# Moving fourteen K masks from GpSimd to VectorE, and making the instruction order with measured GpSimd lengths

## The chip, the cores and the metric

The kernel runs on one core of one Trainium2 chip. A time is the device time of one execution in microseconds (us). Most executions of one kernel agree within some tenths of a per cent. The profile is one further look at an execution, taken by the hardware profiler; its span is a little shorter than the device time (284.9 us against 286.6 for the kernel before).

Names in the profile: PE is TensorE's matmuls, PEld its weight loads, DVE is VectorE, ACT is ScalarE, POOL is GpSimd, SP is SyncE. L738 is line 738 of the kernel.

## The reference

The input x is 2048 x 512. Two branches read it and a gate mixes them:

```python
g = sigmoid((x * gate_w).sum(-1, keepdims=True))
a = attention(x)        # 32 heads of 16, in 4 segments of 512 rows, each segment causal,
                        # plus a recurrent memory M, z carried from segment to segment, then @ wo
b = (relu(x @ W_gate) * (x @ W_up)) @ W_down      # 1792 hidden columns
out = g * a + (1 - g) * b
```

Inside a segment the attention is `softmax(q @ k.T * scale + mask) @ v`. The dense products (q, k, v, gate, up, down, wo) are most of TensorE's work. The attention needs every engine: scores on TensorE, exponentials on ScalarE, the causal triangle masks on GpSimd, the product with v ("PV") on TensorE again, then transposes and scaling on VectorE.

## The kernel before

The program is written as a list of small operations. Each has a table "engine: assumed length in us", dependencies and buffers. A list scheduler in the kernel's own source simulates the engines with these lengths and fixes the order in which instructions are issued. At run time each engine executes its instructions strictly in that order. A wrong length makes no wrong result; it makes an order in which an engine stands at an instruction that is not ready while later ones are.

The odd and even heads of a pair share 32 partitions, so K is masked twice, once for each (`r` is 0 for the even heads, 1 for the odd):

```python
for r, mc in ((0, mcole), (1, mcol)):
    def f(e, r=r, mc=mc):
        (nc.vector if e == "DVE" else nc.gpsimd).tensor_scalar(                     # L552, L553
            k2.t[:, :, r, :], k.t[:].rearrange("p (b k) -> p b k", k=64), mc[:, 0:1], None, ALU.mult)
    o_k2[s, c].append(op(f"k2{s}{c}{r}",
                         {"DVE": 0.45} if r == 0 or (s == 0 and c < 2) else {"POOL": 0.8}, f, ...))
```

There are 4 segments `s` and 4 groups `c` of eight heads, so 16 odd masks; two are on VectorE already, 14 on GpSimd.

The triangle masks come after the exponentials (two instructions a part, 128 parts, 256 instructions):

```python
for off in offs:
    for r in range(2):
        v = eb_.t[64 * r:64 * r + 64, :, off:off + 64]
        nc.gpsimd.affine_select(out=v, in_=v, compare_op=ALU.is_ge, fill=0.0, ...)   # L738
m = op(f"m{s}{c}.{n}", {"POOL": 0.8 * len(parts)}, f, deps=[b], ...)
```

PV waits for all of these masks of its unit. Its result goes through VectorE's transposes and products; in segments 1 to 3 a GpSimd add then joins it with the memory part, and VectorE transposes the sum:

```python
Oa.t[:] = Oa.t[:] + Ob.t[:]     # L895: op "ad", {"POOL": 0.8} for 11 of 12, the last {"DVE": 0.5}
nc.vector.transpose(dst.t[:], Oa.t[:]...)                                            # L899
```

PSUM holds one score tile and four tiles G that all other matmuls share. VectorE and ScalarE empty them. So when VectorE stands at an instruction, TensorE soon stands too, for want of a free G.

The softmax here doesn't subtract the row's maximum and nothing guards it: scores larger than these inputs give would overflow.

## Time and profile before

| | before |
|---|---|
| median, three runs | 286.34 us (284.88 to 286.56) |
| profiled span | 284.9 us |
| TensorE busy | 265.1 us, 93% |
| GpSimd busy | 210.7 us, 74% |
| ScalarE, VectorE busy | 194.0 us, 179.7 us |
| mean granted TensorE clock | 0.982 |

The profile's page for the kernel before: busy time and share of the span by engine, then busy tenths and granted clock in 40 slices of 7.1 us.

```profile
PE 265.1 (93%) x2626; PEld 119.0 (42%) x2661; DVE 179.7 (63%) x402; ACT 194.0 (68%) x188; POOL 210.7 (74%) x481
...
PE   8999999978979989999799997999999899999995
...
POOL 9299889989889886799858988648988886636000
PEclk9999999997999999999899997999999999999999
```

TensorE is the busiest, but its row has holes, and the clock row drops where some holes are. GpSimd is at 8 or 9 tenths in most slices of the middle. (35 matmuls fewer than weight loads are listed: some records are missing, so TensorE's idle time of 284.9 - 265.1 = 19.8 us is overstated, by 2 to 3 us as an estimate: the waits view has 2.6 us of idle time marked "issue".)

The groups of instructions of the kernel before (line, engine, operation, output <- input, shapes, count | busy us, mean ns of one | idle before them and what ended it):

```profile
L738 POOL TENSOR_SCALAR_AFFINE_SELECT E<-E 64x256 bf16<-64x256 bf16 x256 | 115.9, 453 | 30.9 <-ACT E L730 16.8
L553 POOL TENSOR_SCALAR K<-KT,mcol 128x512 bf16<-128x512 bf16 x14 | 22.2, 1591 | 6.0 <-ACT KT L509 5.1
L895 POOL TENSOR_TENSOR O<-O,O 128x512 bf16<-128x512 bf16 x11 | 12.8, 1161 | 4.6 <-DVE O L873 4.0
...
L553 DVE TENSOR_SCALAR K<-KT,mcole 128x512 bf16<-128x512 bf16 x16 | 7.2, 447 | 0.5 <-ACT KT L509 0.5
L553 DVE TENSOR_SCALAR K<-KT,mcol 128x512 bf16<-128x512 bf16 x2 | 0.7, 348 | 0.0
```

The same mask takes 1591 ns on GpSimd and 348 ns on VectorE. The scheduler believed 0.8 us for it, 0.8 us for two triangle masks that take 2 x 453 ns, and 0.8 us for an add that takes 1161 ns.

Who waited for whom, the kernel before (us in total, times, longest):

```profile
DVE oT L899 <- POOL O L895: 18.4, 10, 3.4
...
PE G L818 <- POOL E L738: 4.0, 4, 2.6
PE G L242 <- DVE T L853: 2.5, 3, 1.0
PE G L242 <- DVE hT L641: 2.0, 1, 2.0
```

The timeline of the kernel before around its longest TensorE gap, GpSimd's queue first (start us, duration us):

```profile
53.39 1.56 POOL L553 TENSOR_SCALAR K<-KT,mcol 128x512 bf16<-128x512 bf16 x1
54.90 0.88 POOL L472 COPY R<-rcol 32x4 f32<-32x4 f32 x4
55.85 2.02 POOL L738 TENSOR_SCALAR_AFFINE_SELECT E<-E 64x256 bf16<-64x256 bf16 x4
57.94 2.32 POOL L472 COPY R<-rcol 32x4 f32<-32x4 f32 x8
...
64.53 1.82 POOL L738 TENSOR_SCALAR_AFFINE_SELECT E<-E 64x256 bf16<-64x256 bf16 x4
64.99 0.37 PE L818 MATMUL G<-E,Vp 64*32 64x256 bf16 x4 [2.64 <-POOL E L738]
```

Here PV waits 2.64 us for triangle masks, which stand in a queue that was never empty. The second kind of gap goes through VectorE:

```profile
137.23 1.15 POOL L895 TENSOR_TENSOR O<-O,O 128x512 bf16<-128x512 bf16 x1
138.41 0.71 DVE L899 STREAM_TRANSPOSE oT<-O 128x512 bf16<-128x512 bf16 x1 [3.44 <-POOL O L895]
139.05 1.85 DVE L641 TENSOR_TENSOR hT<-G,rg 128x512 bf16<-128x512 f32 x3
139.75 0.64 PE L242 MATMUL G<-xT,wg_sb 128*128 128x512 bf16 x2 [1.99 <-DVE hT L641]
```

VectorE stands 3.44 us at a transpose behind GpSimd's late add; the product hT behind it, which would free a G, is late; TensorE stands 1.99 us.

The granted clock falls to half at three places of this trace, for 3.4 us each (from 65.1, 140.2 and 174.3 us): right after the two longest gaps, 2.64 and 1.99 us, and after a stretch of shorter ones, 0.95, 0.16 and 0.21 us. Stretches of 2 us around the first (busy us of PE, PEld, DVE, ACT and POOL with instruction counts, then clock, DMA share, GB/s):

```profile
62.00:64.00 2.00, 0.35 (x24) 0.09 (x1) 0.37 (x1) 2.00 (x3) 1.70 (x7) 1.00 0.18 37
64.00:66.00 2.00, 0.90 (x32) 0.60 (x31) 0.00 (x0) 0.46 (x1) 1.71 (x6) 0.77 0.14 28
66.00:68.00 2.00, 1.78 (x18) 0.50 (x12) 1.75 (x3) 0.00 (x0) 1.76 (x5) 0.50 0.00 0
```

TensorE works again from 65 us, at half clock up to 68.5 us. Over the whole span a mean clock of 0.982 is (1 - 0.982) x 284.9 = 5.1 us of full-speed work lost.

### The profile page before, as it was taken

The numbers are of one execution on the slowest core, as the hardware profiler recorded it, in microseconds if no ns is written. First come the engines' busy times: TensorE is split into PE (matmuls) and PEld (weight loads), VectorE is DVE, ScalarE is ACT, GpSimd is POOL, SyncE is SP. The second block draws the span as 40 slices with busy tenths as digits, with TensorE's granted clock in tenths as the row PEclk, the third lists the DMA queues.
The fourth block names the chain that finished last, engine by engine and source line by source line (L and its number), as shares of the span: only waits on it lengthen the run. The fifth ranks groups of instructions, "written<-read, shape, count | busy, mean of one in ns | idle before, by whom it ended". The sixth has DMA issues, their size and how long they took to land.

```text
span 284.9 us, 6734 instructions
## 1 busy us (share of the span) xinstructions
PE 265.1 (93%) x2626; PEld 119.0 (42%) x2661; DVE 179.7 (63%) x402; ACT 194.0 (68%) x188; POOL 210.7 (74%) x481
## 2 busy tenths in 40 slices
PE   8999999978979989999799997999999899999995
PEld 6444444423444434444245433344434444444444
DVE  1498778975685527799477941848697645456601
ACT  3599879983857565999678562788868756777010
POOL 9299889989889886799858988648988886636000
PEclk9999999997999999999899997999999999999999
DMA  6992990023600000001531000000000001100011
GB/s 185 290 226 61 317 305 9 2 51 72 101 5 18 21 18 21 0 2 21 141 45 21 21 18 21 20 0 2 3 0 2 2 1 39 38 2 0 2 37 39
DMA packets 27600, 15.52 MB, mean 54 GB/s; under 512 B 13616, under 2 KB 27568, under 8 KB 27568
## 3 DMA queue, kind: packets, MB, share of 16 engines
q1 hardware_dynamic: 26736, 14.63, 20.0%
q10 hardware_dynamic: 832, 0.46, 0.5%
q8 instruction: 21, 0.34, 0.5%
q14 instruction: 11, 0.09, 0.1%
HBM read 9.84 MB, written 2.10 MB: 42 GB/s over the span
## 4 chain that ended last, share of the span: by engine, by line
PE 58%; POOL 27%; issue 6%; DVE 5%; ACT 3%; POOLq 0%; DVEq 0%; ACTq 0%
PE G L242 44%; POOL E L738 12%; PE S L716 5%; PE G L818 4%; POOL R L472 3%; POOL CM L792 3%; POOL K L553 2%; POOL O L895 2%; ACT E L730 2%; PE G L240 2%; PE S L402 1%; POOL M L618 1%; DVE T L853 1%; PE G L285 1%; DVE hT L641 1%
## 5 line engine op out<-in xcount | busy, mean ns | idle before, releaser
L730 ACT ACTIVATE E<-S 128x2048 bf16<-128x2048 f32 x72 | 135.0, 1875 | 48.7 <-PE S L716 44.6
L738 POOL TENSOR_SCALAR_AFFINE_SELECT E<-E 64x256 bf16<-64x256 bf16 x256 | 115.9, 453 | 30.9 <-ACT E L730 16.8
L242 PE MATMUL G<-xT,wg_sb 128*128 128x512 bf16 x207 | 56.0, 381 | 3.5 <-DVE hT L641 2.0
L242 PE MATMUL G<-xT,wu_sb 128*128 128x512 bf16 x202 | 55.5, 383 | 3.0 <-DVE T L853 1.5
L242 PE MATMUL G<-wd_sb,hT 128*128 128x512 bf16 (+1 forms) x231 | 54.6, 373 | 0.8 <-issue 0.6
L641 DVE TENSOR_TENSOR hT<-G,rg 128x512 bf16<-128x512 f32 x56 | 37.7, 677 | 12.5 <-ACT rg L637 6.2
L853 DVE STREAM_TRANSPOSE T<-G 128x512 f32<-128x512 f32 x44 | 30.4, 702 | 17.7 <-PE G L818 14.5
L637 ACT ACTIVATE rg<-G 128x512 bf16<-128x512 f32 x56 | 32.7, 596 | 11.9 <-PE G L242 11.5
L242 PEld LDWEIGHTS <-hT 128*128 128x128 bf16 x238 | 22.3, 99 | 24.7 <-issue 4.0
L242 PEld LDWEIGHTS <-wg_sb 128*128 128x128 bf16 x214 | 19.6, 98 | 28.4 <-issue 7.3
L242 PEld LDWEIGHTS <-wu_sb 128*128 128x128 bf16 x214 | 19.5, 99 | 26.6 <-issue 6.2
L716 PE MATMUL S<-QT,K 32*128 32x192 bf16 (+7 forms) x512 | 29.0, 291 | 0.8
L553 POOL TENSOR_SCALAR K<-KT,mcol 128x512 bf16<-128x512 bf16 x14 | 22.2, 1591 | 6.0 <-ACT KT L509 5.1
L818 PE MATMUL G<-E,Vp 64*32 64x128 bf16 (+7 forms) x512 | 21.0, 299 | 3.2 <-POOL E L738 3.0
L899 DVE STREAM_TRANSPOSE oT<-O 128x512 bf16<-128x512 bf16 x16 | 11.3, 708 | 18.5 <-POOL O L895 18.4
L818 PE MATMUL G<-E,VS 64*32 64x64 bf16 (+7 forms) x512 | 20.7, 298 | 1.1 <-POOL E L738 1.0
L716 PEld LDWEIGHTS <-K 32*128 32x128 bf16 x512 | 8.4, 92 | 30.3 <-issue 29.5
L242 PE MATMUL G<-wo_sb,oT 128*128 128x512 bf16 (+1 forms) x66 | 16.8, 366 | 0.2 <-issue 0.2
L818 PEld LDWEIGHTS <-Vp 64*32 64x32 bf16 x512 | 12.6, 95 | 10.1 <-issue 7.2
L242 PE MATMUL G<-xT,wk_sb 128*128 128x512 bf16 x63 | 16.4, 380 | 0.2 <-issue 0.2
L678 DVE TENSOR_SCALAR os<-G,ngcol 128x512 bf16<-128x512 f32 (+1 forms) x9 | 6.2, 684 | 16.3 <-PE G L242 16.3
L895 POOL TENSOR_TENSOR O<-O,O 128x512 bf16<-128x512 bf16 x11 | 12.8, 1161 | 4.6 <-DVE O L873 4.0
(93 smaller groups left out, 307.6 us busy)
## 6 DMA issues: line engine op xcount, KB each, us to landing
out_dram<-os SPq DMA_DIRECT2D x15, 128.0 KB, 1.7
wd_sb<-in_B_W_down_dram SPq DMA_DIRECT2D x1, 1792.0 KB, 13.5
xn<-in_A_x_dram SPq DMA_DIRECT2D x3, 512.0 KB, 4.2
wg_sb<-in_B_W_gate_dram SPq DMA_DIRECT2D x2, 512.0 KB, 5.3
wu_sb<-in_B_W_up_dram SPq DMA_DIRECT2D x2, 512.0 KB, 6.4
wg_sb<-in_B_W_gate_dram SPq DMA_DIRECT2D x3, 256.0 KB, 6.9
wu_sb<-in_B_W_up_dram SPq DMA_DIRECT2D x3, 256.0 KB, 7.1
wk_sb<-in_A_wk_dram SPq DMA_DIRECT2D x1, 512.0 KB, 4.7
```

The lines of the kernel that those rows point to most:

```text
L242: nc.tensor.matmul(out_ap, lhsT=lhsT, rhs=rhs, start=start, stop=stop)
L472: nc.gpsimd.tensor_copy(R[s][32 * j:32 * j + 32, :, k], rcol[32 * k:32 * k + 32, cols])
L553: (nc.vector if e == "DVE" else nc.gpsimd).tensor_scalar(k2.t[:, :, r, :], k.t[:].rearrange("p (b k) -> p b k", k=64), mc[:, 0:1], None, A ...
L637: nc.scalar.activation(rg.t[:], g.t[:], ACT.Relu)
L641: nc.vector.tensor_tensor(h.t[:], u.t[:], rg.t[:], ALU.mult)
L716: nc.tensor.matmul(sp.t[:, j, off:off + w], lhsT=K2[s, cc].t[rows, kb, :, :].rearrange("p r k -> p (r k)"), rhs=QT[s, cc].t[rows, L - w:L] ...
L730: nc.scalar.activation(eb_.t[:], sp.t[:], ACT.Exp, scale=SCALE)
L738: nc.gpsimd.affine_select(out=v, in_=v, compare_op=ALU.is_ge, fill=0.0, base=0, pattern=[[0, 4], [1, 64]], channel_multiplier=-1)
L818: nc.tensor.matmul(gs[r].t[32 * j:32 * j + 32, L - w:L], lhsT=v, rhs=src.t[rows, j, off:off + w], start=(kb == 0), stop=(kb == 7), tile_po ...
L853: nc.vector.transpose(T.t[:].rearrange("p b e -> p (b e)"), g.t[:])
L895: (nc.vector if e == "DVE" else nc.gpsimd).tensor_tensor(Oa.t[:], Oa.t[:], Ob.t[:], ALU.add)
L899: nc.vector.transpose(dst.t[:], Oa.t[:].rearrange("p b r e -> p (b r e)"))
```

## The change

The intent: take the 14 masks off the engine that is behind, and plan the two remaining kinds of GpSimd work with lengths near the measured ones, so that the order fits what happens.

```diff
-            o_k2[s, c].append(op(..., {"DVE": 0.45} if r == 0 or (s == 0 and c < 2) else {"POOL": 0.8}, f,
+            o_k2[s, c].append(op(..., {"DVE": 0.45}, f,
...
-            m = op(f"m{s}{c}.{n}", {"POOL": 0.8 * len(parts)}, f, deps=[b], key=kf, uses=[eb_])
+            m = op(f"m{s}{c}.{n}", {"POOL": 0.95 * len(parts)}, f, deps=[b], key=kf, uses=[eb_])
...
-            deps = [op(f"ad{s}{c}", {"DVE": 0.5} if ... else {"POOL": 0.8}, f, ...)]
+            deps = [op(f"ad{s}{c}", {"DVE": 0.5} if ... else {"POOL": 1.18}, f, ...)]
```

All three edits also change the order, on every engine, because the scheduler sees other lengths.

More of the change, by code (lines that the diff above doesn't have):

```diff
@@ L554, in f @@
                     k2.t[:, :, r, :], k.t[:].rearrange("p (b k) -> p b k", k=64), mc[:, 0:1], None, ALU.mult)
-            o_k2[s, c].append(op(f"k2{s}{c}{r}", {"DVE": 0.45} if r == 0 or (s == 0 and c < 2) else {"POOL": 0.8}, f,
+            o_k2[s, c].append(op(f"k2{s}{c}{r}", {"DVE": 0.45}, f,
                                  deps=[b, o_mcol], key=a.key, cls=1, alloc=[k2] if r == 0 else [],
@@ L895, in f @@
                 (nc.vector if e == "DVE" else nc.gpsimd).tensor_tensor(Oa.t[:], Oa.t[:], Ob.t[:], ALU.add)
-            deps = [op(f"ad{s}{c}", {"DVE": 0.5} if (s, c) == (NSEG - 1, NC - 1) else {"POOL": 0.8}, f, deps=outs[0][0] + outs[1][0], key=k0 + PU, uses=[Oa, Ob])]
+            deps = [op(f"ad{s}{c}", {"DVE": 0.5} if (s, c) == (NSEG - 1, NC - 1) else {"POOL": 1.18}, f, deps=outs[0][0] + outs[1][0], key=k0 + PU, uses=[Oa, Ob])]
         def f(e):
```

## The prediction

> **What bounds the kernel now.** TensorE: the page gives PE 265.1 of 284.9 us (93%), GpSimd 210.7 (74%), ScalarE 194.0 (68%), VectorE 179.7 (63%). PE is not the whole story: the chain that ended last is 58% PE and 27% GpSimd. In ten-microsecond windows GpSimd is 8.6 to 9.3 us busy in nearly every window from 20 to 110 us and again in 120 to 140, 150 to 170, 200 to 220 us: there it is saturated, and the fixed instruction order of every engine was made with GpSimd lengths that are too short. Modelled against the groups view: triangle mask 0.8 per part against 2 x 453 ns; odd-head K mask 0.8 against 1591 ns; add 0.8 against 1161 ns. Over 128 parts, 14 masks and 11 adds GpSimd has about 28 us more work than the order assumes.
>
> PE's idle time of 19.8 us is 1.1 at the start, about 3.3 at the end and some 15 inside. The timeline shows these inner gaps that lead back to GpSimd: 2.64 us at 62.4 (PV waits for a triangle mask), 1.00 + 0.37 at 105 to 107 and 1.99 at 137.8 (VectorE had stood 3.44 us at the output transpose behind GpSimd's add, PE wanted the buffer), 1.3 at 172 to 174 (PV on masks), 0.66 at 207.7, 0.85 at 224.8: 8.8 us. After three of them the granted clock falls to 0.5 to 0.6 for some 4 us; the mean clock 0.982 is 5 us of lost PE time. The Trainium skill, "TensorE: Matmul & The Clock Gate", § What's actually happening, says that the gate follows recent activity; the trace agrees in that the drops come right after the long gaps. So about 14 us can be won at most.
>
> **What the change does.** It removes 14 GpSimd masks, 22.3 us (1591 ns each), and adds 14 VectorE masks at 348 ns (measured on the two already there; 447 ns mean of the even ones): 5 to 6 us. VectorE goes to about 184, GpSimd to about 189 us. The Trainium skill, "SBUF — State Buffer", § Who interferes with whom, says that GpSimd shares a port pair with VectorE's two-port and two-input operations and the second waits. The trace agrees: even-head masks took 782 ns beside a GpSimd mask against 319 at best, triangle masks up to 966 against 406. So the new masks will give perhaps 3 us back to GpSimd as waits, and the vanished 1.6 us ones free VectorE. Matmul count is unchanged. Two lengths in the order rise to 0.95 and 1.18, so PV and the output transposes should be put later, with dense matmuls ahead of them.
>
> **Critical path.** Of 22 us only what ends PE gaps counts. I take half of the 14 us: about 7 us, since a new order will make some gaps elsewhere (projection windows at 40 to 60 and 120 to 130 us have VectorE at 9.1 to 9.3 of 10 already).
>
> **Predicted: 279.0 us**, range 272.5 to 285.5. Faster by over 2% (below 280.6) 0.60, within 2% 0.36, slower 0.04.
>
> **What would show it.** GpSimd busy near 190 us; the mask group on VectorE x30 at 350 to 450 ns; PE waits on triangle masks below 1.5 us in all; VectorE's wait at the output transpose for the add (18.4 us now) at most 10; PE idle near 14 us; mean clock 0.99. PE's matmul groups unchanged in mean.
>
> **What would make it wrong.** New gaps from VectorE in the projection stages (PE waiting on hT or T for a PSUM buffer); triangle masks lengthened by more than 10% by the shared ports; ScalarE's exponentials, 135 us, pacing the attention so that freed GpSimd time is only idle; a bad turn of the order, since one changed length moves every later instruction.

## The result, and the profile after

| | before | after |
|---|---|---|
| median, four runs each | 286.45 us | 271.58 us (271.25 to 271.98) |
| ratio | | 0.9493, 95% interval 0.9457 to 0.9529 |
| profiled span | 284.9 us | 269.9 us |
| TensorE busy, idle | 265.1, 19.8 us | 262.2, 7.7 us |
| GpSimd, VectorE busy | 210.7, 179.7 us | 188.7, 185.9 us |
| granted clock | 0.982 | 1.000 |

A ratio here is the mean time of one kernel's fast runs over the mean of the other's fast runs of the same rounds, so it is not quite the ratio of the quoted medians. The change made the kernel 5.1% faster. The predicted direction was right; the time lies below the predicted range of 272.5 to 285.5.

The page of the kernel after, same rows as above:

```profile
PE 262.2 (97%) x2658; PEld 117.2 (43%) x2658; DVE 185.9 (69%) x415; ACT 194.7 (72%) x189; POOL 188.7 (70%) x467
...
PE   8999999999999999999999999799999999999995
...
POOL 9268889888689887579557988875878876535000
PEclk9999999999999999999999999999999999999999
```

Its groups:

```profile
L738 POOL TENSOR_SCALAR_AFFINE_SELECT E<-E 64x256 bf16<-64x256 bf16 x256 | 114.0, 445 | 38.4 <-ACT E L730 24.0
L895 POOL TENSOR_TENSOR O<-O,O 128x512 bf16<-128x512 bf16 x11 | 12.8, 1164 | 4.0 <-DVE O L873 3.3
...
L553 DVE TENSOR_SCALAR K<-KT,mcol 128x512 bf16<-128x512 bf16 x16 | 6.8, 422 | 0.0
L553 DVE TENSOR_SCALAR K<-KT,mcole 128x512 bf16<-128x512 bf16 x16 | 6.3, 395 | 0.2 <-ACT KT L509 0.2
```

Its waits, and the one long TensorE gap that is left in its timeline:

```profile
DVE oT L899 <- POOL O L895: 13.4, 6, 3.9
...
PE G L242 <- DVE hT L641: 1.9, 1, 1.9
```

```profile
170.74 1.02 PE L242 MATMUL G<-xT,wg_sb 128*128 128x512 bf16 x4 [1.90 <-DVE hT L641]
```

The row of PE's waits for GpSimd's triangle masks (`PE G L818 <- POOL E L738`) is gone altogether. Summed over every row of the waits view in which a matmul waits for another engine or a DMA, leaving out the 1.1 us at the start, TensorE waited 10.9 us before and 3.0 us after. (The before view has a further 2.6 us marked "issue", which stand where records may be missing.) The span fell by 15.0 us: as listed, 12.1 us less idle time of TensorE and 2.9 us less busy time. But the 35 missing records count as idle time before; with the 2 to 3 us that they are worth put back, the split is about 9 to 10 us less idle and 5 to 6 us less busy, the latter with the same number of matmuls in the program and a clock that no longer drops.

GpSimd now waits for ScalarE's exponentials (24.0 us in the triangle masks' row, 16.8 before): it has caught up. The two-microsecond gap that is left is of the second kind, the transpose behind a late add.

### The profile page after: what moved, and what is told of

Read it like the earlier page. It is cut to its first block, busy times and chain, and to the rows that moved or that the text cites. A ratio compares the mean times of both kernels' runs of the same rounds, so it can differ in the third digit from the quotient of the medians.

```text
span 269.9 us, 6743 instructions
## 1 busy us (share of the span) xinstructions
PE 262.2 (97%) x2658; PEld 117.2 (43%) x2658; DVE 185.9 (69%) x415; ACT 194.7 (72%) x189; POOL 188.7 (70%) x467
## 4 chain that ended last, share of the span: by engine, by line
PE 83%; POOL 9%; DMA 3%; DVE 2%; issue 1%; ACT 1%; SPq 0%; POOLq 0%
PE G L242 66%; PE S L716 8%; PE G L818 6%; POOL E L738 5%; DMA wk_sb<-in_A_wk_dram 2%; PE G L240 2%; POOL R L472 1%; DMA xn<-in_A_x_dram 1%; POOL O L895 1%; POOL M L618 1%; ACT E L730 1%; PE G L601 1%; POOL CM L792 1%; DVE hT L641 0%; POOL Z L619 0%
## 5 line engine op out<-in xcount | busy, mean ns | idle before, releaser
L738 POOL TENSOR_SCALAR_AFFINE_SELECT E<-E 64x256 bf16<-64x256 bf16 x256 | 114.0, 445 | 38.4 <-ACT E L730 24.0
L242 PE MATMUL G<-xT,wg_sb 128*128 128x512 bf16 x214 | 57.2, 380 | 1.9 <-DVE hT L641 1.9
L242 PE MATMUL G<-xT,wu_sb 128*128 128x512 bf16 x214 | 56.8, 380 | 0.0
L853 DVE STREAM_TRANSPOSE T<-G 128x512 f32<-128x512 f32 x44 | 30.5, 704 | 15.5 <-PE G L818 12.9
L899 DVE STREAM_TRANSPOSE oT<-O 128x512 bf16<-128x512 bf16 x16 | 11.3, 704 | 13.4 <-POOL O L895 13.4
L589 POOL COPY VS<-Vp 64x256 bf16<-64x256 bf16 x32 | 13.4, 418 | 8.7 <-DVE Vp L507 7.2
L818 PE MATMUL G<-E,Vp 64*32 64x128 bf16 (+7 forms) x512 | 19.1, 284 | 0.1
L818 PE MATMUL G<-E,VS 64*32 64x128 bf16 (+7 forms) x512 | 18.4, 284 | 0.4 <-DVE hT L641 0.4
L678 DVE TENSOR_SCALAR os<-G,ngcol 128x512 bf16<-128x512 f32 (+1 forms) x10 | 6.9, 688 | 16.3 <-PE G L242 16.3
L472 POOL COPY R<-rcol 32x4 f32<-32x4 f32 x64 | 14.1, 220 | 3.0
L895 POOL TENSOR_TENSOR O<-O,O 128x512 bf16<-128x512 bf16 x11 | 12.8, 1164 | 4.0 <-DVE O L873 3.3
## 6 DMA issues: line engine op xcount, KB each, us to landing
wd_sb<-in_B_W_down_dram SPq DMA_DIRECT2D x1, 1792.0 KB, 12.7
```

Of the source, the lines that this page charges most:

```text
L242: nc.tensor.matmul(out_ap, lhsT=lhsT, rhs=rhs, start=start, stop=stop)
L472: nc.gpsimd.tensor_copy(R[s][32 * j:32 * j + 32, :, k], rcol[32 * k:32 * k + 32, cols])
L589: nc.gpsimd.tensor_copy(VS[s].t[64 * r:64 * r + 64, t, 0:H // 2 * HP].rearrange("p (h v) -> p h v", v=HP)[:, :, 0:DH], src[:, :, r, 0:DH])
L818: nc.tensor.matmul(gs[r].t[32 * j:32 * j + 32, L - w:L], lhsT=v, rhs=src.t[rows, j, off:off + w], start=(kb == 0), stop=(kb == 7), tile_po ...
L853: nc.vector.transpose(T.t[:].rearrange("p b e -> p (b e)"), g.t[:])
L895: (nc.vector if e == "DVE" else nc.gpsimd).tensor_tensor(Oa.t[:], Oa.t[:], Ob.t[:], ALU.add)
```

## The experiments

The change does two things at once, and a third (a new order) follows from both. The theories:

- **W**, later **Q**: GpSimd's queue was late because it had too much work; any 22 us less, or more, of it show in the time.
- **O**: the order was bad because it was planned with wrong lengths; a better order is the gain.
- **D**: the scores waited for the odd-head masks themselves.
- **P**: long GpSimd instructions keep VectorE from ports that both use.

The same instruction order can be issued with one group of operations on another engine, because the operation chooses its engine when it is issued. In experiments 1, 2, 5, 6, 7, 8, 9 and 12 the order of TensorE's and ScalarE's instructions was compared with that of the kernel it came from and is the same; so is that of VectorE and GpSimd, apart from the instructions moved or added. All twelve gave correct results. "Waits" is the sum defined above.

| run | order of | masks on | median us | before, same rounds | ratio, 95% interval | GpSimd busy | waits |
|---|---|---|---|---|---|---|---|
| before | before | GpSimd | 286.45 | | 1 | 210.7 | 10.9 |
| after | after | VectorE | 271.58 | 286.45 | 0.9493 (0.9457-0.9529) | 188.7 | 3.0 |
| e1 | before | VectorE | 272.93 | 285.14 | 0.9565 (0.9493-0.9637) | 189.7 | 3.0 |
| e2 | after | GpSimd | 282.57 | 285.14 | 0.9912 (0.9855-0.9970) | 209.6 | 10.1 |
| e3 | new: lengths alone | GpSimd | 281.98 | 285.14 | 0.9889 (0.9835-0.9943) | 210.3 | 9.5 |
| e4 | new: masks alone | VectorE | 273.66 | 285.14 | 0.9597 (0.9545-0.9649) | 188.6 | 3.2 |
| e5 | after + long dummies | VectorE | 287.42 | 285.78 | 1.0069 (1.0014-1.0124) | 213.7 | 12.7 |
| e6 | after + short dummies | VectorE | 287.08 | 285.78 | 1.0059 (1.0013-1.0106) | 209.7 | 12.9 |
| e7 | after, masks twice | VectorE | 272.21 | 285.78 | 0.9540 (0.9498-0.9583) | 188.7 | 2.9 |
| e8 | before, adds on VectorE | GpSimd | 276.88 | 285.78 | 0.9704 (0.9660-0.9748) | 198.6 | 5.5 |
| e9 | after, adds on VectorE | VectorE | 268.35 | 284.54 | 0.9431 (0.9399-0.9464) | 175.6 | 0.2 |
| e10 | new: adds planned on VectorE | VectorE | 270.36 | 284.54 | 0.9502 (0.9469-0.9535) | 176.7 | 1.4 |
| e11 | new: adds on either | VectorE | 271.29 | 284.54 | 0.9529 (0.9497-0.9562) | 180.8 | 3.2 |
| e12 | after + half the dummies | VectorE | 277.32 | 284.54 | 0.9746 (0.9712-0.9780) | 201.7 | 6.4 |

Below, "wins" or "loses" is the difference of the two medians of one row, and runs of different calls are set beside each other by these differences. On this scale the change wins 286.45 - 271.58 = 14.9 us. The kernel before itself had medians from 284.54 to 286.45 us in the four calls, so differences of different calls agree only within about 2 us.

### e1: the work moved, the order kept

```diff
# in the kernel before
-                (nc.vector if e == "DVE" else nc.gpsimd).tensor_scalar(
+                nc.vector.tensor_scalar(
```

> The instruction order of the kernel before on TensorE, ScalarE and GpSimd, unchanged; only the 14 odd-head K masks are issued to VectorE at their old places. Theory W (the GpSimd work itself held TensorE up; 22 us of it is gone, whatever the order): at most 275 us, GpSimd near 189 us busy, inner TensorE gaps under 6 us. Rival O (the order was made with GpSimd lengths that are too short, and a better order is what gains): at least 281 us, several of the old gaps still there. Both half: 276 to 280.

Measured: 272.93 us, 12.2 us won, without moving one instruction of TensorE or ScalarE. GpSimd is at 189.7 us. The PV of the 2.64 us gap above (65 us there) runs through without a gap here. Waits view, the row of PV behind triangle masks (4.0 us before):

```profile
PE G L818 <- POOL E L738: 1.2, 3, 0.8
```

Theory W's forecast is met (at most 275 us); most of the gain needs no new order.

### e2: the order changed, the work kept

```diff
# in the kernel after
-                (nc.vector if e == "DVE" else nc.gpsimd).tensor_scalar(
+                (nc.vector if r == 0 or (s == 0 and c < 2) else nc.gpsimd).tensor_scalar(
```

> The instruction order of the kernel after on TensorE, ScalarE and the rest, but the 14 odd-head K masks are issued to GpSimd at their places. Theory W: at least 281 us, GpSimd near 211 us busy, the gaps come back. Rival O: at most 276 us.

Measured: 282.57 us, 2.6 us won (0.9 to 4.1 by the interval). With e1 this makes a square: old order and old work 0, work alone 12.2, order alone 2.6, both 14.9. Within the uncertainty the two effects add up (12.2 + 2.6 = 14.8). Waits view:

```profile
PE G L242 <- DVE hT L641: 4.6, 3, 1.9
...
PE G L818 <- POOL E L738: 2.7, 3, 2.3
```

Both kinds of gap are back.

### e3 and e4: each edit alone, with the order that it makes

```diff
# e3, in the kernel before                  # e4, in the kernel after
-  {"POOL": 0.8 * len(parts)}               -  {"POOL": 0.95 * len(parts)}
+  {"POOL": 0.95 * len(parts)}              +  {"POOL": 0.8 * len(parts)}
-  {"POOL": 0.8}     (the add)              -  {"POOL": 1.18}    (the add)
+  {"POOL": 1.18}                           +  {"POOL": 0.8}
```

> The two lengths of the change (0.95 per part and 1.18) in a newly made order, the masks left on GpSimd with their old length 0.8. Theory W: 281 to 288 us, as GpSimd still does 211 us of work. Rival O: 271 to 278 us.

> The masks on VectorE in a newly made order, with the old lengths 0.8 and 0.8. Theory W: 270 to 275 us, GpSimd near 189 us. Rival O: 279 us or more, because triangle masks and adds, 128 and 11 of them, are still planned too short.

Measured: the lengths alone win 3.2 us (281.98), the masks alone 11.5 us (273.66). The part of the lengths is 3 us on either side: 3.2 without the masks, 14.9 - 11.5 = 3.4 with them. Theory W predicted both. O was not wrong in kind, but its share is about a fifth (3.2 us, 1.6 to 4.7 by the interval).

### e5 and e6: useless GpSimd work, long and short

```diff
# in the kernel after, at the place of each of the 14 masks; nothing waits for these
+ e5: for n in (416, 96): nc.gpsimd.tensor_scalar(dmy[:, 0:n], gwrep[:, 0:n], mc[:, 0:1], None, ALU.mult)
+ e6: for _ in range(8):  nc.gpsimd.tensor_copy(dmy[0:32, :], dsrc[0:32, :])
```

(e5 needed 832 bytes a partition; one spare CM buffer was given up for it, which renumbers a buffer and moves no instruction.)

> The kernel after, its order unchanged, and GpSimd does 14 pieces of useless work at the places of the masks, each of about 1.6 us in two instructions (416 and 96 columns), written to a tile nobody reads. Theory Q (GpSimd's queue: any 22 us of work in it make its triangle masks and adds late): 279 to 284 us, as with the masks on GpSimd in this order (282.6). Rival D (the scores waited for the odd-head masks themselves): at most 274 us. Rival P (the long GpSimd instructions hold the ports that VectorE needs): like Q here, but the next run stays low.

> The same useless GpSimd time in 8 copies of 32x4 values, some 0.2 us each (1.6 us a piece, 22 us in all), so that VectorE can get in between. Theory Q: within 1.5 us of the run with the long ones. Rival P: at most 275 us and at least 4 us below it. Rival D: at most 274 us.

Measured: 287.42 and 287.08 us, worse than the kernel before: of the 14.9 us won, 14.9 + 1.6 = 16.5 and 14.9 + 1.3 = 16.2 us are lost again, although nothing waits for a dummy's result. That rules out D. The two are 0.34 us apart, so whether GpSimd is occupied by 28 long instructions or by 112 short ones makes no difference that matters: P fails too. It is the queue. Both losses are larger than expected. In e5 a piece was longer than planned (2 x 964 ns, 27.0 us in all, not 22); in e6 the copies were 23.1 us and stood 6.6 us idle before them. e5 and e6, groups of the dummies (they are issued from L554):

```profile
L554 POOL TENSOR_SCALAR dmy<-gwrep,mcol 128x416 bf16<-128x416 bf16 (+1 forms) x28 | 27.0, 964 | 2.5
```

```profile
L554 POOL COPY dmy<-dsrc 32x4 f32<-32x4 f32 x112 | 23.1, 206 | 6.6
```

The loss of e6 beyond e2's (16.2 against 12.3 us in the same order, for about the same busy time) may come from that idle time; no run tells.

### e7: more VectorE work

```diff
# in the kernel after: the 14 moved masks are written a second time
+ nc.vector.tensor_scalar(k2.t[:, :, r, :], <same input>, mc[:, 0:1], None, ALU.mult)
```

> The kernel after, its order unchanged, with the 14 moved masks done twice on VectorE, which gives it 5 to 6 us more work, near 192 us in all. If VectorE is pressed in the projection stages, as the prediction feared when it took half of the gain: at least 274.5 us. If VectorE had room: at most 273 us.

Measured: 272.21 us, 1.3 us worse than the change (0.6 by the medians alone; the intervals of the two ratios overlap), with VectorE at 189.8 us. Fourteen more masks on VectorE cost about a microsecond at most; fourteen pieces on GpSimd cost 12 to 16. VectorE had room, also in the projection stages.

### e8: another group of GpSimd work taken away

```diff
# in the kernel before, order kept, K masks still on GpSimd
-  (nc.vector if e == "DVE" else nc.gpsimd).tensor_tensor(Oa.t[:], Oa.t[:], Ob.t[:], ALU.add)
+  nc.vector.tensor_tensor(Oa.t[:], Oa.t[:], Ob.t[:], ALU.add)
```

> The kernel before, its order unchanged, masks still on GpSimd; the 11 adds (12.8 us of GpSimd) are issued to VectorE instead. Theory Q, gain in step with the GpSimd time removed (12.2 us won for 22.3 us in the order before): about 278 us, range 275 to 280. Rival D: at least 283 us.

Measured: 276.88 us, 8.9 us won for 12.8 us of adds. Masks are not special (D fails again). The 2.64 us gap behind the triangle masks stays, while VectorE no longer stands at the transpose; adds seem worth a little more per microsecond; that VectorE stood right behind them may be why. The row of PV behind triangle masks (4.0 us before) in e8:

```profile
PE G L818 <- POOL E L738: 3.0, 3, 2.6
```

### e9, e10, e11: the adds too

```diff
# e9, kernel after, order kept:  as e8
# e10, kernel after, new order:  the add {"DVE": 0.5}
# e11, kernel after, new order:  the add {"DVE": 0.5, "POOL": 1.18}, the last as before
```

> The kernel after, its order unchanged, with the 11 adds also issued to VectorE: GpSimd about 176 us, VectorE about 190. TensorE of the kernel after has only some 2.4 us of inner gaps left, so if TensorE is now the bound, at most 2.4 us can be won: 269 to 271.5 us. If GpSimd still paced it at half a microsecond per microsecond removed (8.9 us won for 12.8 in the order before): 263 to 266 us.

> As the run before it, but the order is made anew with the adds planned on VectorE at 0.5. Bound by TensorE: 268.5 to 271.5 us. GpSimd still pacing: 266 us or less.

> The order made anew with each add left free to go to VectorE (0.5) or GpSimd (1.18). Bound by TensorE: 268.5 to 271.5 us, like the run before it within 1 us.

Measured: 268.35, 270.36 and 271.29 us. e9 is the best kernel here, 16.2 us below before where the change is 14.9. It was not timed in the same rounds as the kernel after, and the intervals of the two ratios overlap slightly (0.9464 and 0.9457), so its lead over the change (1.3 us by the differences, 3.2 by the medians alone) is likely rather than shown. Its page:

```profile
PE 261.9 (98%) x2658; PEld 117.4 (44%) x2658; DVE 189.7 (71%) x426; ACT 194.6 (73%) x189; POOL 175.6 (66%) x456
```

TensorE's idle time is 266.6 - 261.9 = 4.7 us, nearly all of it start and end (1.1 and 3.2 us); the waits sum to 0.2 us. Hardly anything is left to win by removing waits inside this set of matmuls. The expectation put e9 at 269 us or more, because it counted only 2.4 us of gaps in the kernel after; the waits view has 3.0. The scheduler did no better when it was told of the move: e10 is 2.0 us slower than e9 in the same rounds, at about the same GpSimd work. So in this one comparison the turn of an order alone was worth two microseconds, and e3's and e4's 3 us for the lengths is not far above it.

### e12: half the dummies

```diff
# as e5, only where c is odd: 7 pieces
```

> The kernel after, its order unchanged, with 7 of the 14 pieces of useless GpSimd work (two long instructions each, 1.93 us a piece in the run with 14, 13.5 us in all). If the loss goes in step with the work (15.8 us for 14 pieces): about 279.5 us. If the kernel after has slack and the loss starts late: at most 276 us.

Measured: 277.32 us, between the two forecasts (279.5 in step, at most 276 with slack), so neither is met. By the differences 14.9 - 7.2 = 7.7 us of the gain are lost for 13.6 us of dummies, against 16.5 us for 27.0 in e5 (0.57 and 0.61 us per microsecond). By the medians alone, as the forecast reckoned, it is 5.7 us against 15.8 (0.42 and 0.59). The dummies of e12:

```profile
L554 POOL TENSOR_SCALAR dmy<-gwrep,mcol 128x416 bf16<-128x416 bf16 (+1 forms) x14 | 13.6, 971 | 1.2
```

A good part of the added work shows in the time already at 13.6 us, though GpSimd's average share in the kernel after is only 70%; whether a little slack is used up first stays open.

## Why the prediction was right or wrong

**Right: what was in the way.** It named GpSimd's late queue as the cause of TensorE's gaps. e1, e5, e8 and e12 show it: with the order held, GpSimd work taken away or added moves the time by 12.2 / 22.3 = 0.55, 16.5 / 27.0 = 0.61, 8.9 / 12.8 = 0.70 and 7.7 / 13.6 = 0.57 us per microsecond (the last is 0.42 by the medians alone).

**Right: the sizes of the work.** GpSimd came to 188.7 us (189 predicted), VectorE to 185.9 (184), the mask group to 422 ns (350 to 450), PE's waits on triangle masks to none (below 1.5). The triangle masks did not get longer (445 against 453 ns), and the matmul groups kept their mean of 380 ns.

**Nearly right: the total that could be won.** The estimate was 8.8 us of gaps and 5 us of clock, about 14; the span fell by 15.0, and with the missing records put back TensorE has 9 to 10 us less idle and 5 to 6 us less busy time, close to both terms. The clock went from 0.982 to 1.000. What the clock is worth by itself is not shown: of the 25 executions of the kernel before that were timed in the experiments' rounds, the 11 with a mean clock of 0.986 or more took 284.1 us on average and the 14 with 0.982 or less 285.7, so 1.7 us for a clock difference of 0.014, where the estimate's rule (0.014 x 285) gives 4.0. That the clock fell because of the gaps is argued from their places alone; no run tested it, and in e1 it fell at 164.5 us with no single gap over 0.78 us in the six microseconds before.

**Wrong: the step "I take half of the 14 us: about 7 us, since a new order will make some gaps elsewhere (projection windows at 40 to 60 and 120 to 130 us have VectorE at 9.1 to 9.3 of 10 already)".** This put 279.0 us where 271.58 was measured. The mechanism was right and this factor was mis-sized: against the ceiling of about 14 us, 14.9 came, so the factor measured about 1 and not one half. Its two reasons fail separately. VectorE was not a limit: giving it the same 14 masks once more cost 1.3 us or less (e7). And the gain did not hang on a new order: the old one kept 12.2 us of it (e1), and the new one brought 2.6 us more rather than costing some (e2). A busy share of 0.9 in a window says that an engine has work, not that others wait for it; in the waits view before, the TensorE waits on VectorE of 1 us or more (1.00 and 1.99) traced back to a transpose that stood for GpSimd.

**Mis-weighted: the lengths.** The prediction opened with 28 us of GpSimd work that the order did not know of. Correcting the two lengths was worth about 3 us (e3, e4), near the 2 us that separate two orders of the same work (e9, e10).

**Missed: two smaller marks.** VectorE's wait for the add was predicted at 10 us at most and is 13.4; TensorE's idle time near 14 us and is 7.7. Waits at the transpose remained without TensorE standing for them; e9 shows that removing them all brings only another 1.3 us by the differences, 3.2 by the medians.

## What to carry to other kernels

Hold the instruction order and move only the work: this one-line experiment separates "too much work" from "bad order", and here it gave 12.2 and 2.6 of 14.9 us. Judge a helper engine not by its share over the span (74% looked harmless) but by whether its queue runs empty and who stands at its results: add a known amount of useless work and see what it costs per microsecond (here about 0.6 on GpSimd, and on VectorE about 0.2 at most, an estimate: 1.3 us for 14 masks of some 0.42 us). Here nearly all gaps of the busiest engine led back to one engine, and nearly all closed when its work was taken away. Before discounting a forecast gain, name the next limit by a wait and not by a busy digit.

## What the Trainium skill lacked or had wrong

- "SBUF — State Buffer", § Who interferes with whom, says that where a two-port VectorE operation and a GpSimd operation meet, the second fully blocks until the first is done. Whether the VectorE masks run in a two-port mode the trace doesn't show; if they do, it differs. The VectorE mask below starts 0.10 us after a GpSimd mask and ends 0.73 us before it: it is long (776 ns, against 319 at best) but not blocked to the end. Two others lay wholly inside a GpSimd mask (from 13.89 and 14.75 us) and took 349 and 347 ns. Spans on GpSimd are rough, but 0.73 us is nearly half of this one. The prediction took the long ones as agreement; what lengthened them was not tested. And long dummies against short ones changed the time by 0.34 us (e5, e6).

```profile
131.82 1.61 POOL L553 TENSOR_SCALAR K<-KT,mcol 128x512 bf16<-128x512 bf16 x1
131.92 0.78 DVE L553 TENSOR_SCALAR K<-KT,mcole 128x512 bf16<-128x512 bf16 x1
```

- "GPSIMD Engine Reference", § 4.1 Engine selection, gives GpSimd as about 2 times slower than VectorE for two inputs and roughly at line rate for one. The runs show 1591 against 348 to 422 ns (3.8 to 4.6 times) for the one-input mask on 128x512 bf16, and 1161 against 458 ns (e9, 2.5 times) for the two-input add.
- "TensorE: Matmul & The Clock Gate", § What's actually happening, has the clock at half after at least one idle window of about 3.4 us. Each drop in the trace before lasted 3.4 us, which agrees. But it fell to 0.50 after a gap of 2.64 us, after one of 1.99 us, and in e1 with no single gap over 0.78 us before it, while the 1.90 us gap of the kernel after left it at 1.00. So the length of the gap alone does not decide here. The stretch after the 1.99 us gap (before), then the one in which the 1.90 us gap ends (after):

```profile
140.00:142.00 2.00, 2.00 (x42) 0.67 (x48) 1.53 (x4) 1.01 (x1) 1.72 (x4) 0.54 1.08 250
170.00:172.00 2.00, 1.26 (x6) 0.48 (x5) 1.97 (x5) 0.20 (x1) 1.77 (x5) 1.00 0.00 0
```

- "Perfetto Trace Analysis", § Identifying the Most-Contended Engine, finds the engine to work on by its occupancy, and for TensorE does not count the matmul busy share as a measure of headroom. Occupancy did point to GpSimd here (74%, the highest besides TensorE), but it did not say what its work costs: 0.4 to 0.7 us per microsecond. No page gives the test used here, useless work added to one queue with the order held (e5, e6, e12).
